# Moving the second P V block of each stretch behind the second q product and o wo in a fused attention kernel

## The chip, the cores and the metric

The kernel runs on one core of one Trainium2 chip, in one launch. The metric is the device time of the whole kernel in microseconds (us). A core has a matrix engine (PE), three engines for elementwise work (DVE, ACT, POOL), an engine that mainly issues DMAs (SP), and 16 DMA engines. Each engine runs its own instructions in the order in which the kernel issues them, and waits at semaphores for the others.

## The reference

The input x has 2048 tokens of 640 features. It is normalised, goes through attention over a window of a key/value cache, and is multiplied by a gate that a small routed feed-forward network (for two chosen tokens) changes. Cut to what matters here:

```python
xn = layernorm(x)                                   # 2048 x 640
q = (xn @ wq).reshape(2048, 32, 192)                # 32 heads of 192
k, v = k_cache[:, -512:], v_cache[:, -512:]         # the last 512 of 2048, for each head
p = softmax(q @ k.T * 192 ** -0.5)                  # 2048 x 512 for each head
o = p @ v                                           # "P V"
s = o.reshape(2048, 32 * 192) @ wo                  # "o wo", 2048 x 640
out = x + s * silu(routed_ffn(xn))
```

Inputs and output are bfloat16.

## The kernel before

The heads are taken in 8 groups of 4 (`GROUP`), each group in two pairs of heads; the tokens in 4 blocks of 512. A step is (group, block of 512 tokens, pair of heads), 64 steps in all. In a step the q product makes three pieces of 128 features by 512 tokens (`q_item`, five matmuls each into one PSUM tile, evacuated by ACT into `qT`). A step has four units m, one for 128 tokens and both heads of the pair; there are 256.

For one unit the scores are 128 tokens by 512 keys for each of two heads (`scores`). DVE takes the row maximum of each head's scores (`row_max`), ACT the exponential into `pexp` with the row sums (`exps`). A DMA issued from SP transposes `pexp` into the ring `pT`, which holds six units (`RP`). P V (`o_products`) is eight matmuls of 192 columns into one PSUM tile `o_ps`; DVE evacuates it and divides by the row sums (`o_scaled`, into the ring `o_sb`). A DMA transposes three units of `o_sb` into `oT` (`o_turned`). o wo (`w_item`) takes 128 tokens and one group of four heads: two halves of six matmuls of 320 columns, each half added by DVE into `s_acc` (the last group multiplies by the gate and writes out).

PSUM has eight banks. Four (`ps_sc`) hold scores, two (`ps_w`) are shared by the scores of one unit and by o wo, and two (`ps_f`) are taken in turn by q products, P V and the small products of the feed-forward network, so that each of these waits until the tile two places before it in the order is evacuated.

The order of work is written out by hand. A prologue (`FIRST`) handles the first 24 units in pairs. Then a loop runs 76 stretches of three units each (`for U in range(HEAD, NU - 2)`), and a tail (`LAST`) does the rest. A stretch first issues the scores of its three units. Then it walks through the list of tokens `STRETCH`, the same for every stretch:

- `M0` to `M5`: the row maxima, two for each unit; `E0`, `E1`, `E2`: the exponentials of one unit each. `E1` also issues the transpose of the first two units, `E2` that of the third. `R`: reciprocals of the row sums of the stretch before.
- `O1`: one P V with its evacuation; `O`: what is left of the P V (one, and then the transpose of the three `o_sb`).
- `q1`: one q product with its evacuation; `q`: what is left. A stretch has two or three q products.
- `W1`: one o wo; `W`: what is left. A stretch has one or two o wo.
- `m`, `n`, `b`: background work (layer norm, routing, feed-forward, gate), where there is some; `l`: loads of weights, keys and values for later.

The three P V of a stretch belong to units whose scores were taken earlier: the first to the third unit of two stretches ago, the second and third to the first two units of the stretch before. So the second and third read `pT` from the transpose that `E1` issued in the stretch before. Stretches follow a pattern of four: three q and one o wo; two and two; two and one; two and two.

Of the kernel before, what the change touches and what calls it, by code (L numbers as in the profile page):

```python
# [21 lines left out]
def kernel(ctx, tc, A_x, A_k_cache, A_v_cache, A_wq, A_wo, B_x, B_w_r, B_w_gate, B_w_up, B_w_down, out):  # L22
# [6 lines left out]
    W = min(4096, max(256, Sk // 4))  # L29
# [292 lines left out]
    def scores(U):  # L322

        ms = units[U]
        tiles = {}
        for m in ms[1:] + ms[:1] if len(ms) == 3 else ms:
            g, t5, pr = steps[m // 4]
            ssl = slice((m % 4) * P, (m % 4 + 1) * P)
            if len(ms) == 3 and m == ms[0]:
                s0, s1 = w_banks()  # L330
            else:
                s0 = ps_sc.tile([P, W], FP32, name="s0", tag="sc")
                s1 = ps_sc.tile([P, W], FP32, name="s1", tag="sc")
            qT, kp = qT_of[m // 4], grp[g]["kT"][:, pr]
            nc.tensor.matmul(s0, lhsT=qT[:, 0, ssl], rhs=kp[:, :, 0, :], start=True, stop=False)  # L335
            nc.tensor.matmul(s1, lhsT=qT[:, 2, ssl], rhs=kp[:, :, 2, :], start=True, stop=False)  # L336
            tiles[m] = (s0, s1)
        for m in ms:
            g, t5, pr = steps[m // 4]
            ssl = slice((m % 4) * P, (m % 4 + 1) * P)  # L340
            s0, s1 = tiles[m]
            qT, kp = qT_of[m // 4], grp[g]["kT"][:, pr]
            nc.tensor.matmul(s0, lhsT=qT[0:64, 1, ssl], rhs=kp[0:64, :, 1, :], start=False, stop=True)  # L343
            nc.tensor.matmul(s1, lhsT=qT[64:128, 1, ssl], rhs=kp[64:128, :, 1, :], start=False, stop=True)  # L344
        return [tiles[m] for m in ms]
# [511 lines left out]
        bg[109 + n].append(fin_pre(n))  # L857


    STRETCH = "M0 M1 R O1 E0 q1 M2 M3 E1 O1 M4 M5 E2 W1 m q1 n W q O b l".split()  # L860
    for token in FIRST:
        first(token)
    def q_until(s):
# [5 lines left out]
    for U in range(HEAD, NU - 2):  # L869
# [13 lines left out]
        tiles = scores(U)  # L883
        for token in STRETCH:
            if token[0] == "M":
# [109 lines left out]
```

## Time and profile before

| | |
|---|---|
| three timed runs | 808.7, 811.0, 809.54 us; median 809.54 |
| the profiled execution's own time | 807.38 us |
| its span, first to last instruction | 805.6 us |
| PE busy in the span | 790.8 us (98%) |
| DVE, ACT busy | 624.1 us (77%), 500.2 us (62%) |
| granted PE clock | 0.999 |
| DMA engines busy | 0.7 to 0.9 of the time in nearly every slice |
| P V (L378) | 2048 matmuls, 211.1 us busy |
| q products (L294) | 945 matmuls, 230.4 us busy |
| o wo (L419) | 1536 matmuls |
| transposes `pT<-pexp` | 169, median 4.3 us from issue to landing |

Matmuls are pipelined, so the duration of one in the profile is longer than the distance from one to the next. An engine's rows show what it did; the chain of work that ended last shows what the end of the kernel had to wait for, step by step. Times in the text are counted from the start of the span, or, where it says so, from the start of a stretch, which is the first matmul of its scores.

### The profile page before, as it was taken

To read this page: it belongs to the slowest core of one execution; us is meant where nothing else is said; L and a number is where in the kernel's file an instruction comes from. 1 tells how busy PE (TensorE), PEld (TensorE's weight loads), DVE (VectorE), ACT (ScalarE), POOL (GpSimd) and SP (SyncE) were. 2 spreads that over 40 slices of the span, in tenths; PEclk is the share of its full clock that TensorE was granted. 3 is DMA by queue.
4 is the path that set the end of the run, shared out by engine and by line. 5 is a ranking of instruction groups with operands and counts; after the bars stand their busy time and mean duration, and the time that the engine had idled before them with its cause. 6 is when DMAs were issued, how large, how long until landed. Compare 5 with 4: busy or idle time off the path is not lost.

```text
span 805.6 us, 15848 instructions
## 1 busy us (share of the span) xinstructions
PE 790.8 (98%) x5776; PEld 483.2 (60%) x5776; DVE 624.1 (77%) x1303; ACT 500.2 (62%) x1281; POOL 217.4 (27%) x175
## 2 busy tenths in 40 slices
PE   8899999999999999999999999999999999999997
PEld 4456566666566665665665666666665565656665
DVE  7988778887787766777776777678888877668895
ACT  5777655665566665566655566557776666556651
POOL 0112000000000000000003899999900002452554
PEclk9999999999999999999999999999999999999999
DMA  8998999999799998899997996788888899897996
GB/s 219 189 176 167 195 203 168 173 174 189 160 203 195 200 198 162 187 199 191 206 184 151 188 199 138 154 174 174 172 159 152 164 183 188 166 156 145 176 156 133
DMA packets 441678, 142.31 MB, mean 177 GB/s; under 512 B 414500, under 2 KB 441256, under 8 KB 441600
## 3 DMA queue, kind: packets, MB, share of 16 engines
q1 hardware_dynamic: 439936, 138.79, 90.0%
q0 software_dynamic: 720, 1.70, 0.8%
q8 instruction: 45, 0.74, 0.4%
q10 hardware_dynamic: 944, 0.82, 0.3%
q14 instruction: 33, 0.27, 0.1%
HBM read 39.98 MB, written 2.62 MB: 53 GB/s over the span
## 4 chain that ended last, share of the span: by engine, by line
PE 89%; DMA 4%; DVE 3%; ACT 2%; issue 1%; DVEq 0%; SPq 0%; ACTq 0%
PE w L419 24%; PE q_ps L294 23%; PE o_ps L378 20%; PE s L336 4%; PE s L335 4%; PE s L343 4%; DMA pT<-pexp 4%; PE w L343 3%; PE w L335 2%; PE w L336 2%; DVE nm L353 2%; ACT pexp L361 1%; PE warm_ps L146 1%; DVE o_sb L393 0%; PE tp L267 0%
## 5 line engine op out<-in xcount | busy, mean ns | idle before, releaser
L361 ACT ACTIVATE pexp<-s,nm 128x512 bf16<-128x512 f32 x358 | 242.3, 684 | 14.9 <-DVE nm L353 10.5
L361 ACT ACTIVATE pexp<-w,nm 128x512 bf16<-128x512 f32 x154 | 104.5, 683 | 229.7 <-DVE nm L353 229.6
L353 DVE TENSOR_REDUCE nm<-s 128x1 f32<-128x512 f32 x358 | 228.6, 679 | 4.5 <-PE s L344 3.7
L294 PE MATMUL q_ps<-xnT,wq_g 128*128 128x512 bf16 x945 | 230.4, 379 | 0.1
L419 PE MATMUL w<-wo_g,oT 128*128 128x320 bf16 x1500 | 224.2, 299 | 0.0
L378 PE MATMUL o_ps<-v_sb,pT 128*128 128x192 bf16 x2048 | 211.1, 246 | 4.6 <-DMA pT<-pexp 3.2
L378 PEld LDWEIGHTS <-pT 128*128 128x128 bf16 x2048 | 169.1, 98 | 74.1 <-issue 36.6
L419 PEld LDWEIGHTS <-oT 128*128 128x128 bf16 x1536 | 148.6, 98 | 58.7 <-issue 0.9
L393 DVE TENSOR_TENSOR o_sb<-o_ps,lsum 128x384 bf16<-128x384 f32 x249 | 135.1, 543 | 55.5 <-PE o_ps L378 54.7
L353 DVE TENSOR_REDUCE nm<-w 128x1 f32<-128x512 f32 x154 | 99.1, 685 | 66.1 <-PE w L344 66.1
L294 PEld LDWEIGHTS <-wq_g 128*128 128x128 bf16 x945 | 91.0, 98 | 80.3 <-issue 1.1
L299 ACT ACTIVATE qT<-q_ps 128x512 bf16<-128x512 f32 x178 | 106.3, 597 | 22.2 <-PE q_ps L294 14.8
L437 DVE TENSOR_TENSOR s_acc<-s_acc,w 128x320 f32<-128x320 f32 x192 | 86.3, 479 | 28.1 <-PE w L419 28.0
L361 ACT ACTIVATION_READ_ACCUMULATOR pexp<-s,nm 128x1 f32 x358 | 72.0, 201 | 0.0
L336 PE MATMUL s<-kT,qT 128*128 128x512 bf16 x179 | 67.8, 379 | 1.4 <-ACT pexp L361 0.9
L335 PE MATMUL s<-kT,qT 128*128 128x512 bf16 x179 | 67.9, 379 | 0.6 <-ACT pexp L361 0.6
L794 POOL TENSOR_SCALAR yh<-y_bc,oh 128x640 bf16<-128x640 bf16 x32 | 60.5, 1892 | 2.9 <-DMA y_bc<-y_d 1.3
L780 POOL DMA_DIRECT2D y<-yp x4 | 2.1, 524 | 214.3 <-ACT yp L774 214.2
L343 PE MATMUL s<-kT,qT 64*128 64x512 bf16 x179 | 53.2, 377 | 0.0
L344 PE MATMUL s<-kT,qT 64*128 64x512 bf16 x179 | 53.2, 377 | 0.0
L343 PEld LDWEIGHTS <-qT 64*128 64x128 bf16 x256 | 17.1, 94 | 48.4 <-issue 38.4
L795 POOL TENSOR_TENSOR xn<-xn,yh 128x640 bf16<-128x640 bf16 x32 | 44.7, 1396 | 2.7
(148 smaller groups left out, 532.7 us busy)
## 6 DMA issues: line engine op xcount, KB each, us to landing
wo_g<-in_A_wo_dram SPq DMA_DIRECT2D x48, 160.0 KB, 2.9
wq_g<-in_A_wq_dram SPq DMA_DIRECT2D x35, 192.0 KB, 2.9
k_raw<-in_A_k_cache_dram SPq DMA_DIRECT2D x32, 192.0 KB, 3.4
v_sb<-in_A_v_cache_dram SPq DMA_DIRECT2D x32, 192.0 KB, 3.2
pT<-pexp SPq DMA_TRANSPOSE x169, 4.3
x_fin<-in_A_x_dram SPq DMA_DIRECT2D x16, 160.0 KB, 2.7
wgu<-in_B_w_gate_dram SPq DMA_DIRECT2D x15, 128.0 KB, 3.1
wgu<-in_B_w_up_dram SPq DMA_DIRECT2D x15, 128.0 KB, 3.1
```

Of the source, the lines that this page charges most:

```text
L294: nc.tensor.matmul(q_ps, lhsT=grp[g]["wq"][:, dc, col0:col0 + P], rhs=xnT[:, t5 * 4:(t5 + 1) * 4, dc, :], start=(dc == 0), stop=(dc == DC ...
L299: nc.scalar.activation(out=qT_of[i][:, c, :], in_=q_ps, func=ACT.Copy, scale=scale)
L335: nc.tensor.matmul(s0, lhsT=qT[:, 0, ssl], rhs=kp[:, :, 0, :], start=True, stop=False)
L336: nc.tensor.matmul(s1, lhsT=qT[:, 2, ssl], rhs=kp[:, :, 2, :], start=True, stop=False)
L343: nc.tensor.matmul(s0, lhsT=qT[0:64, 1, ssl], rhs=kp[0:64, :, 1, :], start=False, stop=True)
L353: nc.vector.tensor_reduce(out=nm_of[U][:, c:c + 1], in_=tiles[c // 2][c % 2], axis=AX.X, op=ALU.max, negate=True)
L361: nc.scalar.activation(out=p_ring[:, slot, hh, :], in_=tiles[a][hh], func=ACT.Exp, bias=nm_of[U][:, c:c + 1], scale=1.0, accum_out=l_of[U] ...
L378: nc.tensor.matmul(o_ps[:, hh, :], lhsT=pT_ring[:, m % RP, hh, j, :], rhs=grp[g]["v"][:, 2 * pr + hh, j, :], start=(j == 0), stop=(j == NJ ...
L393: nc.vector.tensor_tensor(out=o_sb, in0=o_ps, in1=ls.unsqueeze(2).to_broadcast([P, 2, Dh]), op=ALU.mult)
L419: nc.tensor.matmul(w_ps[:, part.start - off:part.stop - off], lhsT=oT_ring[:, (8 * b + 4 * (c // 3) + u + 1) % RT, c % 3, :], rhs=wo_g[:, ...
L437: nc.vector.tensor_tensor(out=s_acc[:, n, cs], in0=s_acc[:, n, cs], in1=w_ps[:, 0:HD], op=ALU.add)
L794: nc.gpsimd.tensor_scalar(out=yh, in0=M["y_bc"][:, j, :], scalar1=M["oh"][:, n, j:j + 1], scalar2=None, op0=ALU.mult)
```

## The change

One `O1` token, that of the second P V, moves from between the two `q1` tokens to behind `W1`. With it go all that it issues: eight matmuls on PE with their weight loads, and the evacuation on DVE. The second `q1`, with its five matmuls and its evacuation on ACT, thereby stands in front of `M4`, `M5` and `E2`, and the background token `m` behind the second P V. No tile, no loop and no operation is added or removed, and the order on SP and POOL stays.

```diff
-    STRETCH = "M0 M1 R O1 E0 q1 M2 M3 E1 O1 M4 M5 E2 W1 m q1 n W q O b l".split()
+    STRETCH = "M0 M1 R O1 E0 q1 M2 M3 E1 q1 M4 M5 E2 W1 O1 m n W q O b l".split()
```

On PE the order after the scores was O1 q1 O1 W1 q1, (W), (q), O, and is now O1 q1 q1 W1 O1, (W), (q), O, where the brackets mark what only some stretches have.

## The prediction

> **What bounds the kernel now.** I read the page first (shares, chain), then the chain of work piece by piece in the steady loop, then the waits, then the timelines of ScalarE (ACT) and VectorE (DVE) in one stretch. From the page:
>
> ```profile
> PE 790.8 (98%) x5776; PEld 483.2 (60%) x5776; DVE 624.1 (77%) x1303; ACT 500.2 (62%) x1281; POOL 217.4 (27%) x175
> ...
> PE 89%; DMA 4%; DVE 3%; ACT 2%; issue 1%; DVEq 0%; SPq 0%; ACTq 0%
> ```
>
> TensorE (PE) is the bound; the only other large part of the chain is DMA, and by line it is `pT<-pexp`, the transposed probabilities. The chain in one stretch in which nothing waits:
>
> ```profile
> 407.10 0.77 PE o_ps L378 x8
> 407.87 1.08 PE q_ps L294 x5
> 408.95 0.66 PE o_ps L378 x8
> 409.61 1.63 PE w L419 x12
> 411.24 1.08 PE q_ps L294 x5
> 412.31 0.66 PE o_ps L378 x8
> ```
>
> Behind the scores stand block after block with no gap: first P V (O1), first q product (q1), second P V (O2), o wo (W1), second q (q2), third P V (O3). The same chain where it does wait:
>
> ```profile
> 375.27 5.30 DMA pT<-pexp
> 380.56 0.05 issue
> 380.61 0.83 PE o_ps L378 x8
> ```
>
> O2 starts at 380.61. Its q1 starts at 378.67 in the timeline, so q1 to O2 takes 1.94 us where 1.08 is normal: 0.86 us of idle PE, because O2 reads the pT of the pair whose exponentials ended in the middle of the stretch before. I took this distance, q1 to O2, for all 76 stretches of the steady loop (84 to 776 us). With the span's clock: 284 us 0.54, 302 us 0.35, 376 us 0.86, 386 us 0.04, 667 us 0.57, 704 us 0.18, 740 us 0.42. Together 2.96 us, all behind a landing of pT. Three more (568 us 0.08, 640 us 0.83, 750 us 0.02) have another cause: there DVE is late with O1's PSUM. The other steps from block to block in the loop keep their usual length but for some 0.5 us in all, background matmuls aside. The waits of the loop say the same by cause (PE and its weight loads overlap, so the lines do not add):
>
> ```profile
> PE o_ps L378 <- DMA pT<-pexp: 1.9, 5, 0.7
> ...
> PEld L378 <- DMA pT<-pexp: 6.2, 9, 1.2
> ```
>
> **The change: what it takes away.** No instruction is added or removed. In each stretch the PE order O1 q1 O2 W1 (q2) O3 becomes O1 q1 q2 W1 O2 O3, with a second W or third q before O3 as now. O2 starts later by a q product and a W, 1.08 + 1.63 = 2.71 us. The transposes it waits for are issued after the previous stretch's second pair of exponentials, which the change does not move. The worst lateness is 0.86 us, so all seven waits go: **-2.96 us**. The other stretches have O2's data 0.1 to 4.2 us ahead of time (landing against O2's start), most often 1.4 to 3.1. The lateness does not pile up: the stretch after a late one is back at 3 to 4 us ahead, but for 376 us, which 386 us (zero) and 395 us (0.6) follow. The three DVE waits stay: PSUM tiles f have two buffers taken in turn, so what stands third, now q2, waits for O1's evacuation exactly as O2 did.
>
> **What moves on ACT.** q2's evacuation (L299) now stands between the second and third pair of exponentials instead of behind them.
>
> ```profile
> 408.98 0.60 ACT L299 ACTIVATE qT<-q_ps 128x512 bf16<-128x512 f32 x1
> 409.48 0.68 ACT L361 ACTIVATE pexp<-s,nm 128x512 bf16<-128x512 f32 x1
> ...
> 410.14 0.69 ACT L361 ACTIVATE pexp<-s,nm 128x512 bf16<-128x512 f32 x1
> ...
> 410.88 0.69 ACT L361 ACTIVATE pexp<-s,nm 128x512 bf16<-128x512 f32 x1
> ```
>
> This stretch begins at 404.89; I count from there. The second pair of exponentials starts at 4.59 and 5.25, so ACT is free at 5.25 + 0.66 = 5.91. q2's products now end at about 5.1, so the evacuation runs at 5.91, the third pair 0.50 later (408.98 to 409.48) at 6.41, ending at 6.41 + 0.68 + 0.68 = 7.77; before it was 7.35. Who waits: the next scores' third and fourth matmuls need the two PSUM banks that this pair frees at 7.09 and 7.77. They start 0.43 and 0.65 into the next stretch, so in the shortest stretch (7.92 us) at 8.35 and 8.57: **0.8 us of cover**, cost 0. The pT of that pair goes out 0.42 us later but is read two stretches on. On SP the order of DMAs is as before; behind this transpose stand the oT transpose, which waits for O3 anyway, and the loads. Cost 0.
>
> **What moves on DVE.** Its order was M2 M3, O2's evacuation, M4 M5, W1's two adds; now M2 M3 M4 M5, adds, O2's evacuation.
>
> ```profile
> 409.64 0.56 DVE L393 TENSOR_TENSOR o_sb<-o_ps,lsum 128x384 bf16<-128x384 f32 x1
> 410.12 1.28 DVE L353 TENSOR_REDUCE nm<-s 128x1 f32<-128x512 f32 x2
> 411.31 0.87 DVE L437 TENSOR_TENSOR s_acc<-s_acc,w 128x320 f32<-128x320 f32 x2
> ```
>
> The last maximum ends at 6.03 instead of 6.51. W1 ends at 6.60, its last add at about 7.24. O2 ends at 7.26, its evacuation runs from 7.46 to 8.0. Next users of PSUM: q3, or O3 where there is one W and two q, needs q2's evacuation (6.5) at 7.26, 0.75 us of cover; O3 behind a q3 needs O2's evacuation (8.0) at 8.34, 0.35 us of cover; a second W needs W1's adds (6.5 and 7.24) at 7.26 and 8.07.
>
> **Where this cover gets thin.** (a) In the last group W1 has a third DVE operation (L444, 0.82 us) that now comes before O2's evacuation; in the one stretch there with three q (750 us) the evacuation ends near 8.6 and O3 wants 8.34: +0.3 us, between 0 and 1.0 (L444 also ran in 1.53). (b) Where background work for DVE (1.6 to 1.9 us) stands before a second W's adds, these end 0.7 us later, near 10.4 (four stretches with L616) and 10.6 (228 us), against the sixth score matmul's 10.63: +0.1, between 0 and 0.5. (c) At 358 us the small gate and up products come behind a P V instead of behind a q; such a change of step took 0.85 instead of 0.66, against 1.17 instead of 1.08: +0.1. Sum of costs +0.5, bounds 0 to 1.6.
>
> **P V next to P V.** In 18 stretches (one W, two q) O2 and O3 become neighbours, 16 short matmuls each with a weight load of 98 ns (L378 PEld). The prologue has this already:
>
> ```profile
> 74.83 1.32 PE o_ps L378 x16
> ```
>
> 16 at 82.5 ns, the same as 0.66 for 8, so cost 0. The Trainium skill, "TensorE: Matmul & The Clock Gate", section "LDWEIGHTS (loading the stationary operand)", speaks against the move: a load takes its columns divided by 1.2 ns, which by that rule is an estimated 107 ns for 128 columns, more than the 82.5 ns of a matmul here. In this trace the loads overlap well enough to hide that.
>
> **Sum.** -2.96 + 0.5 = **-2.5 us** on the profiled execution, whose own time is 807.38 (span 805.6 and 1.8 around it): 804.9. The timed runs are 808.7 to 811.0, median 809.54, so 2.2 us above the profiled one, and no view shows where. PE in the loop waits for little besides these landings, and seven further stretches have O2's data less than 0.65 us ahead; if the transposes land a little later in other executions, the surplus is partly of this kind. It could as well be the prologue's loads. I credit 0.6 of 2.2 us: **-3.1 us, 806.4 us**. If none of it, 807.0; if all, 804.9.
>
> **Rivals.**
> 1. The gain does not show (0.28): timed runs hold fewer of these waits than the profile, or the time comes back at a later landing (oT, or the next pT), since the DMA engines are 80 to 90 per cent busy in most slices. For it: seven waits in 76 is a matter of luck. Against: the slack after a late stretch recovers. Time 807 to 810, middle 809.
> 2. ACT becomes the bound at the third pair (slower, 0.07). Place: the scores' fourth matmul, waiting for the bank that the last exponential frees. It decides if ACT runs over 0.8 us later than I set it. At 1.2 us late the 18 shortest stretches would lose 0.4 each, 7.2 us, less the gain of 2.5: 814.2. For it: the 62 per cent of ACT is tight in a 7.92 us stretch (six exponentials and two evacuations take some 5.3 us of it, and the first pair cannot begin before 2.54). Against: in every such stretch the second pair started between 4.59 and 4.60.
> 3. Neighbouring P V blocks are paced by weight loads (0.03): 16 x 98 = 1.57 instead of 1.32 us in 18 stretches, +4.5 us, 811.5. The row of the prologue speaks against it. The rule named above gives this direction.
>
> **Numbers.** The forecast has 0.62 (804 to 808), rival 1 0.28, rival 2 0.07, rival 3 0.03. 0.3 per cent, 2.4 us, is about what a measurement of this kernel can tell from no change. Of the forecast's 0.62, 0.56 lies beyond 2.4 us; 0.03 of rival 1's share I leave to its lower end, 807.0, as faster. Rival 3's 811.5 is 0.24 per cent up, mostly within the bound. Faster 0.59, same 0.33, slower 0.08. The range reaches from all of the timed surplus gone and no new cost, with a margin for the runs' own spread of 2.3 us, to rival 1's end: 803.8 to 810.0.
>
> **What would show it.** In the profile after: no wait of L378 for `DMA pT<-pexp` in the loop; q2 to W1 1.08 and W1 to O2 1.63 in all stretches; ACT's third pair ending near 7.77; the wait at 640 us now in front of a q product, if DVE is late again. Wrong if the scores (L335, L336) wait for `ACT pexp`, if 16 P V matmuls take more than 1.35 us, or if pT waits remain.

## The result and the profile after

The changed kernel takes 806.36 us (median of six runs, 805.1 to 806.71) against 809.45 us for the kernel before (six runs, 808.7 to 811.0): a ratio of 0.9958, interval 0.9945 to 0.9971, 3.1 us or 0.4 per cent faster. The profiled execution has a span of 804.4 us and an own time of 806.13.

The page, busy time and the chain that ended last:

```profile
PE 790.8 (98%) x5776; PEld 484.2 (60%) x5776; DVE 641.5 (80%) x1303; ACT 487.1 (61%) x1281; POOL 218.6 (27%) x175
...
PE 93%; DVE 3%; DMA 2%; ACT 1%; issue 0%; DVEq 0%; ACTq 0%; SPq 0%
```

PE does the same work in the same busy time. DMA's share of the chain falls from 4 to 2 per cent; what is left of it lies ahead of the loop's second stretch and in the tail (one transpose, issued at 789 us). A stretch is named by the time at which it starts. The chain in the stretch at 376 us, which stood still for 0.86 us before (start us, us, what):

```profile
378.37 0.77 PE o_ps L378 x8
379.14 2.16 PE q_ps L294 x10
381.30 1.63 PE w L419 x12
382.93 0.66 PE o_ps L378 x8
```

O1, two q products as one run of ten matmuls, o wo, O2: no gap, no landing. The loop's waits of PE, from the second to the last stretch (who, for whom: us in all, times, longest):

```profile
PE q_ps L294 <- DVE o_sb L393: 0.5, 1, 0.5
PE o_ps L378 <- DVE o_sb L393: 0.3, 1, 0.3
```

No wait for `DMA pT<-pexp` is left in these stretches; in the loop's first one O1 waits 0.40 us (0.23 before) for a pT of the prologue. The pT that O2 reads lands 1.6 to 6.6 us before O2 could start, where it was 0.8 us late to 4.2 us early. The q product that waits 0.62 us for O1's evacuation stands at 639 us, where O2 waited before. The 0.3 us are those of the third P V at 748 us. The view gives less than the steps between blocks, which are 0.62 and 0.46 us over their usual length.

The most useful measure, called the loop's time below, runs from the start of the second stretch of the loop to the end of its last (75 stretches), since it leaves out the prologue. It was 682.63 us before and is 679.84 now: **2.79 us less**. The prologue and first stretch took 94.11 us instead of 92.91. Of these 1.20 us, 1.02 are there already at the first score matmul (13.38 instead of 12.36 us), where no changed instruction has run. With 0.34 us more behind the loop, this is why the two profiled executions differ by only 1.25 us in their own times.

### The profile page after: what moved, and what is told of

Same layout as the page of the kernel before. It is cut to its first block, busy times and chain, and to the rows that moved or that the text cites. A ratio compares the mean times of both kernels' runs of the same rounds, so it can differ in the third digit from the quotient of the medians.

```text
span 804.4 us, 15844 instructions
## 1 busy us (share of the span) xinstructions
PE 790.8 (98%) x5776; PEld 484.2 (60%) x5776; DVE 641.5 (80%) x1303; ACT 487.1 (61%) x1281; POOL 218.6 (27%) x175
## 4 chain that ended last, share of the span: by engine, by line
PE 93%; DVE 3%; DMA 2%; ACT 1%; issue 0%; DVEq 0%; ACTq 0%; SPq 0%
PE w L419 25%; PE q_ps L294 25%; PE o_ps L378 21%; PE s L336 5%; PE s L335 5%; PE s L343 5%; PE w L343 3%; PE w L336 2%; PE w L335 2%; DMA pT<-pexp 1%; DVE nm L353 1%; ACT pexp L361 1%; DMA k_raw<-in_A_k_cache_dram 1%; DMA wq_g<-in_A_wq_dram 1%; DVE o_sb L393 0%
## 5 line engine op out<-in xcount | busy, mean ns | idle before, releaser
L353 DVE TENSOR_REDUCE nm<-s 128x1 f32<-128x512 f32 x358 | 222.6, 680 | 4.5 <-PE s L344 3.6
L294 PE MATMUL q_ps<-xnT,wq_g 128*128 128x512 bf16 x945 | 221.7, 379 | 0.5 <-DVE o_sb L393 0.5
L378 PE MATMUL o_ps<-v_sb,pT 128*128 128x192 bf16 x2048 | 208.0, 246 | 2.9 <-DMA pT<-pexp 2.1
L437 DVE TENSOR_TENSOR s_acc<-s_acc,w 128x320 f32<-128x320 f32 x192 | 92.8, 487 | 35.4 <-PE w L419 32.5
L361 ACT ACTIVATION_READ_ACCUMULATOR pexp<-s,nm 128x1 f32 x358 | 77.1, 215 | 0.0
```

The lines of the kernel that those rows point to most:

```text
L294: nc.tensor.matmul(q_ps, lhsT=grp[g]["wq"][:, dc, col0:col0 + P], rhs=xnT[:, t5 * 4:(t5 + 1) * 4, dc, :], start=(dc == 0), stop=(dc == DC ...
L353: nc.vector.tensor_reduce(out=nm_of[U][:, c:c + 1], in_=tiles[c // 2][c % 2], axis=AX.X, op=ALU.max, negate=True)
L361: nc.scalar.activation(out=p_ring[:, slot, hh, :], in_=tiles[a][hh], func=ACT.Exp, bias=nm_of[U][:, c:c + 1], scale=1.0, accum_out=l_of[U] ...
L378: nc.tensor.matmul(o_ps[:, hh, :], lhsT=pT_ring[:, m % RP, hh, j, :], rhs=grp[g]["v"][:, 2 * pr + hh, j, :], start=(j == 0), stop=(j == NJ ...
L437: nc.vector.tensor_tensor(out=s_acc[:, n, cs], in0=s_acc[:, n, cs], in1=w_ps[:, 0:HD], op=ALU.add)
```

## The experiments

Line numbers are those of the kernel before; in the two kernels with late transposes the later ones are larger by 7 (L385 is P V).

**The changed kernel again, and the kernel before twice more.** No edit.

> The changed kernel once more, unaltered. Theory (the gain is the time that the second P V, O2, spent waiting for the landing of its pT; the move gives that landing 2.71 us more): the loop again has no wait of P V for pT worth naming, the time is 806.4 +- 0.7 us and 3.1 +- 0.7 us below the kernel before. Rival (luck: the first two profiles only differ by chance in when transposes landed): the difference to the kernel before shrinks to under 1.5 us, or pT waits of some tenths are back in the loop.

Measured: 805.84 us against 809.18, ratio 0.9958 (0.9944 to 0.9972). The loop took 679.83 us, within 0.01 of the first profile. O1 of the first stretch waited 0.65 us for a pT of the prologue; behind it there is no pT wait. The gain stands.

> The kernel before, unaltered, for a second profile. Theory: its loop again has pT waits in front of O2 and in the same region of stretches (those with many loads), 2 to 5 us in all; if the timed runs' surplus over the first profiled execution (some 2 us) is of this kind, the waits come to 4 to 5 us here when this execution's own time is near 809. Rival (the surplus lies in the prologue's loads): the loop is again 682.6 us from its second to its last stretch and the prologue takes 2 us more.

> A third profile of the kernel before, with the same expectations as the second: with the time of this execution the loop from the second to the last stretch should move (theory), or the prologue (rival).

Measured: own times 807.89 and 808.68 us, loops 683.17 and 683.19 us. The pT waits in front of O2 are back in nearly the same stretches: 3.6 and 3.2 us in six and seven of them, 1.33 and 1.03 at 376 us. So the place of the waits follows from the kernel, and their size varies by some tenths. The time at which the second stretch starts (92.9, 93.1, 93.5 us in the three profiles) orders the three as their own times do. Both the theory and the rival explain a part of the spread; neither the 4 to 5 us nor a prologue longer by 2 us was seen.

**Only q2 moves up; O2 stays.**

```diff
-E1 O1 M4 M5 E2 W1 m q1 n W
+E1 O1 q1 M4 M5 E2 W1 m n W
```

> Only the second q product moves: PE order O1 q1 O2 q2 W1 O3. On ACT its evacuation comes before the third pair of exponentials, as in the changed kernel; O2 stands where it stood. Theory: O2 starts at the same moment of a stretch as in the kernel before (3.89 us after the first score matmul), so its waits for pT stay, 2 to 5 us in the loop, and the time is that of before, 809.4 us (808.5 to 810.5). Rival A (the gain comes from ACT's new order, the evacuation of q2 between the exponentials): 806.4 us.

Measured: 822.47 us, ratio 1.0160 (1.0144 to 1.0176). Both expectations miss: it is 13 us slower. PE and ACT in one stretch (start us, us, engine, line, operation):

```profile
414.60 1.24 PE L294 MATMUL q_ps<-xnT,wq_g 128*128 128x512 bf16 x5
415.68 0.82 PE L378 MATMUL o_ps<-v_sb,pT 128*128 128x192 bf16 x8
416.52 0.59 PE L294 MATMUL q_ps<-xnT,wq_g 128*128 128x512 bf16 x2
```

```profile
415.88 0.60 ACT L299 ACTIVATE qT<-q_ps 128x512 bf16<-128x512 f32 x1
```

The x2 is where the window ends; the block is five matmuls. q2 starts 0.84 us after O2, where a q product behind a P V usually starts after 0.67. Its PSUM tile is the one two places back, q1's, which ACT empties until 416.48. This wait occurs in 72 stretches, 12.8 us in all, and it is new: in the kernel before, o wo stands between O2 and q2 and covers it. O2 still waits: the steps from q1 to O2 exceed their usual length by 4.5 us in 8 stretches, 2.1 us of it in four stretches behind a landing of pT and 2.5 in four behind DVE. Take the 12.8 us off and about the kernel before is left, 809.7. So ACT's new order, with q2's evacuation between the exponentials, seems to bring nothing by itself, but this run shows it only by subtraction; the run with earlier data below decides it.

**O2 moves by one q product, not by a q product and o wo.**

```diff
-E1 O1 M4 M5 E2 W1 m q1 n W
+E1 q1 M4 M5 E2 O1 W1 m n W
```

> O2 moves behind the second q product but stays in front of o wo: PE order O1 q1 q2 O2 W1 O3, so O2 has 1.08 us more instead of 2.71. Theory: the worst lateness seen before was 0.86 us, so nearly all waits go: at most 0.3 us of pT waits left in the loop, 806.4 us (805.5 to 807.3); DVE evacuates O2 before the o wo adds, so the 0.46 us that the changed kernel loses in front of the third P V at 748 us goes too. Rival B (the gain needs o wo between, for instance because the waits of other executions are longer than 1.1 us): 807.5 to 809.

Measured: 806.9 us, ratio 0.9970 (0.9961 to 0.9979), loop 681.68. Two pT waits are left, 0.41 and 0.09 us, at 385 and 375 us; three more stretches have less than 0.7 us to spare. That is the theory's size and place, a little larger. But the wait at 748 us did not just go: DVE's lateness now costs a q product 0.64 us at 748 and O2 0.65 at 767, and a second o wo waits 0.35 at 449 us. The 1.08 us would nearly do against the landings; the loop is still 1.84 us longer than with 2.71.

**Earlier data, order of before.** The first two units' probabilities get a transpose each instead of one together.

```diff
-        n = 1 if a == 2 or U >= NU - 3 else 2
+        n = 1 if a == 2 or U >= HEAD else 2
```

> The order of PE, DVE and ACT is that of the kernel before; in the loop each unit's probabilities get a transpose of their own, issued after their own exponentials, instead of one for the first two units after the second pair. O2's data is issued some 1.9 us earlier (its exponentials end near 4.1 instead of 6.0 us of the stretch); SP issues 75 more transposes. Theory: O2's waits go without any move, 806.4 us (805.5 to 808), unless the additional transposes crowd the DMA queue; then waits appear at other places and are to be seen there. Rival A (order on ACT or DVE) and rival C (the order of blocks on PE itself is faster): 809.4 us, as before.

Measured: 806.65 us, ratio 0.9970 (0.9959 to 0.9980); its loop is 679.92 us, 0.08 from the changed kernel's. The waits of its loop:

```profile
PE o_ps L378 <- DVE o_sb L393: 0.7, 1, 0.7
PE o_ps L378 <- DMA pT<-pexp: 0.2, 1, 0.2
```

One landing is still late, by 0.40 us at 376 us, where loads hold SP until 7.75 us into the stretch. The order of PE, ACT and DVE is that of before, and the gain is there all the same. This decides against order as the cause (rivals A and C): what counts is when O2's pT lands against when O2 wants it.

**Late data, both orders.** The third unit's transpose goes ahead of the first two's, whose own is then issued 3.26 us later in the order of before (median 9.32 instead of 6.06 us into the stretch) and 3.12 us later in the changed order.

```diff
+        late = HEAD <= U < NU - 3
         n = 1 if a == 2 or U >= NU - 3 else 2
...
+        if late and a < 2:
+            return
+        turns = [(a, n)] + ([(1, 2)] if late else [])
```

`turns` lists the transposes to issue: the third unit's, then that of the first two. A loop behind these lines issues them.

> The order of the kernel before, but the transpose of the third unit is issued ahead of that of the first two, so that the pT that O2 reads is issued some 2.8 us later (after the third pair of exponentials, 7.5 us into the stretch, and one transpose of 1.3 us on SP, instead of 6.06). Theory: taking 2.8 to 3.3 us off the slack that each stretch showed, with a wait in one stretch giving its length to the next, the loop loses 56 to 74 us more: 865 to 885 us. Rival A and C (order on ACT, DVE or PE): the lateness costs both orders alike, so this one stays some 3 us above the run late_after.

> The same late transposes in the changed order. The third pair of exponentials ends 0.4 us later here, so the pT comes 3.2 to 3.7 us later than in the changed kernel, whose smallest slacks were 1.6 to 3.2 us. Theory: waits of 7 to 14 us in 10 to 15 stretches: 813 to 820 us, 50 us or more below late_before: the move buys 2.71 us of tolerance in each stretch. Rivals A and C: within some 3 us of late_before.

Measured: 869.76 us in the order of before, ratio 1.0756 (1.0727 to 1.0785), and 809.56 us in the changed order, ratio 1.0005 (0.9994 to 1.0016). The waits of P V in the loop, the order of before first:

```profile
PE o_ps L385 <- DMA pT<-pexp: 48.8, 40, 2.5
```

```profile
PE o_ps L385 <- DMA pT<-pexp: 1.5, 3, 0.6
```

By the steps between blocks, O2 waits 59.2 us in 52 stretches in the one and 2.6 us in 4 in the other. The loops took 744.88 and 683.66 us: nearly the same lateness costs 61.9 us against the mean loop of the kernel before in one order, and 3.8 us against the changed kernel's in the other. Not all of the 61.9 us is waiting: in four stretches (651, 672, 695 and 818 us) the granted PE clock fell to half for 3.4 us, and o wo took 2.6 to 3.2 us there instead of 1.63; with the blocks beside it that is some 6.5 us in all. In the changed order the clock did not fall in the loop.

The expectation for the first holds (865 to 885). That for the second was too high (813 to 820). Taking 3.12 us off the slacks of the changed kernel (its smallest were 1.6, 1.9, 2.0, 2.2) leaves 11 stretches late by 8.4 us in all, as expected. But the landings did not all move by 3.12 us. For the stretch at 376 us the transpose had already gone out late in the changed kernel, 7.54 us into the stretch before. It was now issued at 9.72, only 2.18 later, and landed in 4.76 us instead of 5.39. Three of the four stretches in which O2 did wait are not among the 11.

**O2 ahead of o wo in the last five stretches only.** On top of the change:

```diff
+        order = STRETCH if U < NU - 7 else "... E1 q1 M4 M5 E2 O1 W1 m n W q O b l".split()
```

> The changed kernel, but with O2 in front of o wo instead of behind it in the last five stretches, where o wo carries a third DVE operation. Theory: the third P V at 748 us no longer waits for O2's evacuation (0.46 us there in both profiles of the changed kernel), and the two waits of a first q product that DVE's late maxima cause (0.62 at 640 and 0.09 at 748 us) stay; the transposes of this region were at most 0.37 us late in the order before, less than the 1.08 us that O2 still gains. Loop 679.4 instead of 679.8 us, time 0 to 0.5 us under the changed kernel, too little to tell in the time itself. Rival (moving O2 ahead of o wo makes DVE late elsewhere, as in the run with O2 ahead of o wo everywhere): the 0.46 us comes back as a wait of the o wo or of a q product.

Measured: 806.29 us, ratio 0.9974 (0.9964 to 0.9985), loop 681.34, 1.5 us longer than the changed kernel's. Of this, 0.6 us lies ahead of the last five stretches, where the two kernels are the same (q products waiting for DVE at 550, 568 and 577 us). The last five take 44.35 us instead of 43.42, 0.9 us more, so the rival is right. The third P V no longer waits, but a q product at 749 us now waits 0.64 us, O2 at 768 us 0.65 us. DVE before the first of them, this kernel and then the changed one:

```profile
749.20 2.09 DVE L444 TENSOR_TENSOR fin_o<-fin_t,s_acc 128x640 bf16<-128x640 f32 x1
751.21 0.55 DVE L393 TENSOR_TENSOR o_sb<-o_ps,lsum 128x384 bf16<-128x384 f32 x1
```

```profile
748.14 1.60 DVE L444 TENSOR_TENSOR fin_o<-fin_t,s_acc 128x640 bf16<-128x640 f32 x1
749.67 0.54 DVE L393 TENSOR_TENSOR o_sb<-o_ps,lsum 128x384 bf16<-128x384 f32 x1
```

The same L444 takes 0.82 us elsewhere. It ends late, and the next stretch's maxima with it. No version run here is faster than the changed kernel by more than the noise.

## Why the prediction was right

The forecast of 806.4 us met 806.36, for the reason given: the waits for pT went and nothing of their size came back. That it was met to 0.04 us is luck, since one of its terms, the 0.6 us of the timed surplus, rested on no row.

- **The waits that go.** -2.96 us in the profile of before; all seven are gone in the profile after, and in its repetition. The other two profiles of the kernel before had 3.6 and 3.2 us of them, so 2.96 was rather low. The worst was 1.33 us there instead of 0.86, still within the 2.71 that the move gives.
- **The waits that stay.** DVE's three, 0.93 us, were to remain. Two remain: 0.62 instead of 0.83 at 639 us, now in front of q2 as said, and 0.09 instead of 0.02 at 748 us; that at 568 us is gone.
- **ACT.** Three lines of the profile after, in the shortest kind of stretch; this one starts at 404.27 us:

```profile
410.18 0.60 ACT L299 ACTIVATE qT<-q_ps 128x512 bf16<-128x512 f32 x1
410.66 0.70 ACT L361 ACTIVATE pexp<-s,nm 128x512 bf16<-128x512 f32 x1
...
411.32 0.71 ACT L361 ACTIVATE pexp<-s,nm 128x512 bf16<-128x512 f32 x1
```

  From the start of the stretch that is 5.91 (as forecast), 6.39 (6.41) and an end at 7.76 (7.77). No score matmul of the loop waits for it; rival 2 is out.
- **DVE.** The last maximum ends at 6.03 as forecast, O2's evacuation starts at 7.46 as forecast. (a) The third P V at 748 us waits 0.46 us where 0.3 stood. (b) The stretches with L616 lose nothing: their second pair of adds ends at 10.43, the forecast's 10.4, against 10.63; that of 228 us holds up the next scores by 0.05, and 0.1 stood for both. (c) At 358 us the stretch is as long as before, 10.38: the P V in front of the small products costs 0.09 more, and the q product no longer pays its 0.09. So (a) cost more than forecast and (b) and (c) less; the costs came to about 0.5 us, as summed.
- **P V next to P V.** A run of 16 in the profile after, same view as above:

```profile
411.03 1.32 PE o_ps L378 x16
```

  It is 1.32 us as in the prologue; rival 3 is out. The rule of the Trainium skill, "TensorE: Matmul & The Clock Gate", section "LDWEIGHTS (loading the stationary operand)", an estimated 107 ns for a load of 128 columns, does not set the pace here: a load's record is 98 ns long in the trace and the pairs follow each other at 82.5 ns.
- **The surplus.** The sum gave -2.5 us, the loop shows -2.79, and the mean of the three loops of before (683.00) less that of the two after (679.84) is -3.16, close to the medians' -3.1. So a further 0.66 us came, about the 0.6 credited, but only in part for the reason given: 0.37 is the longer loop of the other two profiles of before, where the pT waits were longer, and 0.29 is the sum's own shortfall, most of it DVE's waits, of which 0.71 us were left and not 0.93. The own times of the profiled executions do not settle it: their means, 807.98 and 805.98 us, are 2.0 us apart, since both executions of the changed kernel reached the loop later. No profiled execution of before had an own time above 808.7 us, and medians of 808.4 to 809.5 were measured: what lies in the slower of its timed runs stays open, and so does why the prologue's time moves by over a microsecond.

Rival 1, the gain given back at a later landing, is answered by the profile after and by the late transposes: the slack of every stretch grew (by 0.1 to 3.6 us), and a transpose issued 3.1 us later still cost only 3.8 us. Its premise was even somewhat stronger than written: the page of before shows the DMA engines busy for 90 per cent or more in 22 of the 40 slices, and for 80 to 90 in 12.

## What to carry to other kernels

When the bounding engine runs nearly without gaps, what a move like this can win lies in the few places where a block's data is later than its turn. List for every such place when the data landed against when the block could start, and move the block by clearly more than the worst of them. Here the worst was 0.86 us in one profile and 1.33 in the next; a move by 1.08 left two waits, and one by 2.71 none. Before moving anything in an order with rotating buffers, count what each moved block's neighbours now find two places back: moving only q2 up cost 13 us through a tile that its old place had hidden. Slack that looks useless in one profile is tolerance: some 3 us of lateness cost 61.9 us in one order and 3.8 us in the other.

## What the runs showed of the hardware

L444, a DVE operation with two SBUF inputs, is held up by a POOL operation that is running, and is not slowed in proportion. It takes 0.82 or 0.83 us where no POOL operation runs beside it. In the last kernel above it starts at 749.20, a hundredth after POOL's L850 (749.19, 1.40 us long), and takes 2.09: the 1.39 until POOL's end and 0.70 more. In the changed kernel it starts at 748.14 beside POOL's L850 of 747.65 to 749.05 and takes 1.60: 0.91 and 0.69. With 0.49 us of POOL's operation left (late transposes, order of before, at 831.80 us) it takes 1.19. So what comes behind POOL's end is the same 0.7 us whatever was left. The Trainium skill, "SBUF — State Buffer", section "SBUF: two separate sides", describes this as an exclusive lock on a port pair that DVE and POOL share, held for a whole instruction. The traces agree, except that the 0.7 us is 0.12 us less than L444 takes alone; why is not shown. The prediction had 1.53 as a bare upper bound for L444 and not this reason.

The granted PE clock fell in the run with late transposes in the order of before: it was 0.50 in four windows of 3.4 us (from 657.6, 678.1, 702.0 and 824.9 us). Around each, PE had just stood idle for 2.0 to 2.5 us; the idle time ended at most 1.1 us before the fall or 0.3 us after it. Idle times of 2.2, 2.1 and 2.5 us at 321, 558 and 799 us were not followed by a fall, so the length of the wait alone does not decide it. What does is not shown.
